# A new table of priorities for the list scheduler of a pooled attention and max-of-three feed-forward kernel

## The chip, the cores and the metric

The kernel runs on one core of a Trainium2 chip. The metric is the device time of one execution in microseconds; the kernel before takes 1482.36 us (median of 3 runs, 1482.32 to 1483.36). The engines are named as in the profile: PE (matmul; PEld loads its weights), DVE (VectorE), ACT (ScalarE), POOL (GpSimd), and SP, whose queue issues nearly all DMAs.

## The reference

Attention with queries averaged in pairs (1152 become 576), for 8 batches of 8 heads with 1152 keys and a head dimension of 64, and then a feed-forward stage on the 4608 resulting tokens, whose hidden layer is the maximum of three products:

```python
q_pool = q.reshape(B, H, S // factor, factor, D).mean(axis=3)
scores = scale * np.matmul(q_pool, k.transpose(0, 1, 3, 2))
scores = scores - np.max(scores, axis=-1, keepdims=True)
attn = np.exp(scores)
attn = attn / (np.sum(attn, axis=-1, keepdims=True) + 1e-09)
attn_out = np.matmul(attn, v)
...
h = np.maximum(np.maximum(x @ w1, x @ w2), x @ w3)
return (h @ w_out).astype(np.float32)
```

The weights w1, w2, w3 and w_out come as 64-bit floats, and the kernel turns each into a high and a low 32-bit part.

## The kernel before

**Units.** Attention is cut into 64 units, numbered d: a pair of heads (four pairs in each of 8 batches) and one half, 288, of its pooled queries. Scores lie with the keys on the partitions, in nine blocks of 128 keys. A unit goes through these steps, whose keys stand in the table of priorities:
- `qk` (lines 538 and 539): PE, four matmuls per key block into `pqk`, of which there are two buffers.
- `cp` (544): ACT copies `pqk` into a third of a tile `s`; a unit has three such tiles, and there are six buffers, so unit d takes those of unit d-2 over.
- `mx` (550, 553): DVE, running maximum `acc` over the key blocks, one buffer.
- `rows`, `red`, `bc` (589, 595, 605): PE transposes `acc` in five blocks (`pmt`), DVE reduces them, PE transposes the result back (`pmb`).
- `sub` (620) on DVE and `exp` (626) on ACT, six pieces each.
- `keys` (639, 641): POOL sums the exponentials over the key blocks into `ksum`, eight additions, in two buffers. The first addition of unit d waits until the `psum` of unit d-2 has read its buffer (line 644).
- `av` (669): PE, product with v into `pav`; `xcopy` (678) brings it to `xr`.
- `psum` (700 and 715 for d below 16, else 683): PE sums `ksum` over the partitions and spreads the reciprocals (`inv`, 690 and 710); `xm` (724 or 693) scales `xr`. `split` (768, 771) makes its high and low part.

**Feed-forward.** The tokens are cut into nine chunks, numbered from 0. Chunk b can start when the attention of its tokens is done; its steps are `mm` on PE, 216 matmuls `ph` (931; six blocks of the hidden layer, three weights each, four parts of 512 rows, three products of high and low parts), `evac` and `hhigh`/`hlow` (950, 952, 959, 962), then 72 matmuls `po` (986) and their copies and stores (1002, 1005). `mm` of all chunks stands in one chain (`tail`). `po` of chunk 0 waits for all six parts of w_out.

**Conversion.** With chunk 0, the weights are loaded (816), converted and stored for the later chunks (877), which fetch them (891). Of 24 conversions, `conv` in the table, 18 are of w1 to w3 (tiles `w0_0` to `w0_17`, four buffers, so `w0_4` waits until chunk 0 has used `w0_0`) and six of w_out (`wo_hi`, `wo_lo`). Each runs on ACT and DVE (831 to 858); the last two operations (861, 864) are POOL's for even numbers and DVE's, in two halves, for odd ones. `ph`, `po`, `psum`, the early `pav` and the conversions share two buffers `ff`.

**Order.** All steps go into a plan, and `arrange` walks through it with a clock for each engine: of the steps that are ready on the engine that is free first, it takes the one of lowest rank, and books an assumed duration. The instructions of each engine are then issued in this order; the chip waits on semaphores wherever a modelled time was too short. A step's rank is, with `at` near the unit's number d,

```python
lambda: at + R[key] + (R.get("first_" + key, 0) if at < 8 else 0) + NUDGE.get(name, 0)
```

and for the feed-forward steps of chunk b, with d the unit behind which it is planned (8, 16, ...) and i the place in the chunk,

```python
lambda: d + R["ffn"] + R[rate] * n * i / 576 + R[key] + NUDGE.get(name, 0)
```

`RANK` has an entry for each kind of step. `NUDGE` shifts single steps: those of units 0 to 19 (`keys.13`), and those of chunks 0 and 1 by eighths of 48 places (`conv.8.9`, `mm.8.3`). From unit 20 and chunk 2 on, `RANK` alone decides.

Of the kernel before, what the change touches and what calls it, by code (L numbers as in the profile page):

```python
# [36 lines left out]
    "qk": -94.8622,  # L37
    "cp": -198.877,
    "mx": -110.1936,
    "rows": -297.5399,  # L40
    "red": -97.7108,
    "bc": -69.2978,
    "sub": 36.0255,
    "exp": -154.9623,
    "keys": -14.5562,
    "av": 14.8431,
    "xcopy": -242.7422,
    "psum": 306.6745,
    "eps": 163.4791,
    "inv": 411.5164,  # L50
    "xm": -165.8669,
    "load": 11.9358,
    "prep": 513.6605,
    "move": 372.9744,
    "split": 31.5471,
    "ffn": -33.8173,
    "rate": 1.0394,
    "mm": 49.1178,
    "fetch": -156.7626,
    "evac": -234.7904,  # L60
    "hhigh": 172.1589,
    "hlow": -152.0307,
    "conv": 478.2091,
    "rate0": 4.4379,
    "first_qk": 87.3127,
    "first_cp": -260.4178,
    "first_mx": 25.0784,
    "first_sub": 35.563,
    "first_exp": 326.0935,
    "first_keys": -44.827,  # L70
    "first_av": 37.0199,
    "first_xcopy": -183.8483,
    "first_psum": -32.0782,
    "first_inv": -61.85,
    "first_xm": -117.3451,
    "first_load": -320.6766,
    "first_prep": -184.3904,
    "first_move": -506.8185,
    "first_split": 49.1161,
# [991 lines left out]
```

## Time and profile before

| | us |
|---|---|
| median of 3 runs | 1482.36 |
| lowest and highest run | 1482.32, 1483.36 |
| span of the profiled execution | 1480.9 |
| PE busy, 8704 matmuls | 1400.6 |
| POOL busy | 1078.7 |
| DVE busy | 1046.1 |
| ACT busy | 904.5 |

The profile gives the span of its execution, from the first to the last instruction, and no time of the whole execution; the median of the runs is 1.5 us above that span. Matmul ends are modelled, so a busy PE is not necessarily PE at its best. "Idle before" an instruction is put down to what ended it; a wait for several things is put down to the last of them. Which engine sets the pace changes during the span, so the tables by stretches say more than the shares.

### The profile page before, as it was taken

The page shows a single profiled execution, that of the slowest core. Times are in us where ns is not written, and L with a number is a line of the kernel's source. Part 1 is how long each engine was busy: PE and PEld are TensorE (multiplying, and loading weights), DVE is VectorE, ACT ScalarE, POOL GpSimd, SP SyncE. Part 2 cuts the span into 40 slices and gives each one's busy share as a digit, 9 for nine tenths or more (in the row PEclk, how much of TensorE's full clock was granted, in tenths as well). Part 3 has the DMA queues.
Part 4 walks back from the last instruction along what each step waited for, and adds up shares of the span by engine and source line. Part 5 has one row for each costly group of instructions (what it writes and reads, how often), then busy time and mean ns, then how long its engine had stood idle before and what let it go on. Part 6 is the DMA issues. An engine that isn't in the chain of part 4 may idle for free.

```text
span 1480.9 us, 24740 instructions
## 1 busy us (share of the span) xinstructions
PE 1400.6 (95%) x8704; PEld 1098.3 (74%) x8704; DVE 1046.1 (71%) x1441; ACT 904.5 (61%) x1464; POOL 1078.7 (73%) x835
## 2 busy tenths in 40 slices
PE   4788999888899999999999999999999999999999
PEld 4566666666567878778777777777777777778999
DVE  4898788989896875577777777877777778761110
ACT  4767766647676766467666676676766766651211
POOL 1888977686887868478887898789878988772210
PEclk9989899988999999999999999999999999999999
DMA  6556446657545665465566656664666556424441
GB/s 184 154 160 187 115 132 181 185 176 229 158 120 158 195 190 170 130 196 169 155 184 180 182 142 177 181 190 139 176 180 187 150 165 184 139 72 157 152 159 60
DMA packets 114762, 240.71 MB, mean 163 GB/s; under 512 B 15440, under 2 KB 75216, under 8 KB 114640
## 3 DMA queue, kind: packets, MB, share of 16 engines
q1 hardware_dynamic: 114064, 238.55, 55.2%
q8 instruction: 70, 1.15, 0.3%
q10 hardware_dynamic: 576, 0.59, 0.2%
q14 instruction: 52, 0.43, 0.1%
HBM read 144.70 MB, written 18.87 MB: 110 GB/s over the span
## 4 chain that ended last, share of the span: by engine, by line
PE 70%; DVE 4%; DMA 2%; issue 1%; POOL 1%; ACT 1%; SPq 0%; ACTq 0%; DVEq 0%
PE ph L931 27%; PE pav L669 13%; PE po L986 10%; PE pqk L538 7%; PE pqk L539 7%; PE pmt L589 2%; PE psum L683 2%; PE pmb L605 2%; DVE acc L553 1%; DMA w<-in_wout_dram 1%; DVE s L620 1%; DMA qq<-qraw 1%; POOL ksum L641 0%; DVE w L834 0%; DVE w L839 0%
## 5 line engine op out<-in xcount | busy, mean ns | idle before, releaser
L641 POOL TENSOR_TENSOR ksum<-ksum,s 128x576 f32<-128x576 f32 x448 | 638.0, 1424 | 28.9 <-ACT s L626 5.8
L931 PE MATMUL ph<-xh,w 128*128 128x512 f32 (+2 forms) x1440 | 464.6, 377 | 5.4 <-DVE hm L952 4.0
L620 DVE TENSOR_TENSOR s<-s,pmb 128x1035 f32<-128x1035 f32 (+1 forms) x384 | 396.9, 1049 | 46.0 <-PE pmb L605 46.0
L544 ACT COPY s<-pqk 128x576 f32<-128x576 f32 x576 | 362.5, 638 | 105.2 <-PE pqk L539 101.4
L538 PE MATMUL pqk<-qq,kc 128*128 128x288 f32 x1152 | 360.0, 327 | 57.1 <-DVE acc L553 35.3
L553 DVE TENSOR_TENSOR acc<-acc,pqk 128x576 f32<-128x576 f32 x448 | 335.3, 748 | 84.5 <-ACT s L544 81.7
L626 ACT ACTIVATE s<-s 128x1035 f32<-128x1035 f32 (+1 forms) x384 | 354.8, 934 | 60.2 <-DVE s L620 57.1
L539 PE MATMUL pqk<-qq,kc 128*128 128x288 f32 x1152 | 333.4, 304 | 0.0
L538 PEld LDWEIGHTS pqk<-qq,kc 128*128 128x128 f32 x1152 | 225.5, 196 | 113.5 <-DVE acc L553 51.7
L669 PE MATMUL pav<-s,v 128*64 128x288 f32 x2304 | 306.8, 419 | 1.8 <-DVE xr L724 1.4
L931 PEld LDWEIGHTS ph<-xh,w 128*128 128x128 f32 x1440 | 263.1, 188 | 45.9 <-DVE hm L952 4.9
L931 PE MATMUL ph<-xl,w 128*128 128x512 f32 (+2 forms) x720 | 268.4, 373 | 0.0
L669 PEld LDWEIGHTS pav<-s,v 128*64 128x64 f32 x2304 | 165.1, 141 | 122.0 <-issue 17.7
L539 PEld LDWEIGHTS pqk<-qq,kc 128*128 128x128 f32 x1152 | 227.9, 198 | 11.2
L962 POOL TENSOR_TENSOR h_lo<-hm,h_hi 128x512 fp32r<-128x512 f32 (+2 forms) x60 | 70.8, 1179 | 149.5 <-ACT h_hi L959 149.5
L639 POOL TENSOR_TENSOR ksum<-s 128x576 f32<-128x576 f32 x64 | 91.9, 1436 | 105.5 <-ACT s L626 103.1
L952 DVE TENSOR_TENSOR hm<-hm,ph 128x512 f32<-128x512 f32 (+2 forms) x120 | 75.4, 628 | 127.5 <-PE ph L931 127.5
L931 PEld LDWEIGHTS ph<-xl,w 128*128 128x128 f32 x720 | 135.8, 189 | 11.8
L595 DVE TENSOR_REDUCE m<-pmt 116x3 f32<-116x384 f32 (+1 forms) x128 | 61.1, 488 | 91.9 <-PE pmt L589 91.9
L434 POOL TENSOR_TENSOR kraw<-kraw 128x1152 fp32r<-128x1152 f32 x31 | 82.9, 2675 | 57.1 <-ACT kraw L430 39.4
L690 DVE RECIPROCAL rs<-rs 128x288 f32<-128x288 f32 (+1 forms) x64 | 96.3, 1506 | 18.5 <-ACT rs L687 18.2
L678 ACT COPY xr<-pav 128x288 f32<-128x288 f32 x64 | 25.4, 398 | 114.8 <-PE pav L669 114.6
(57 smaller groups left out, 1288.9 us busy)
## 6 DMA issues: line engine op xcount, KB each, us to landing
w<-w_split SPq DMA_DIRECT2D x144, 512.0 KB, 3.4
kc<-kraw SPq DMA_DIRECT2D x384, 96.0 KB, 2.3
qq<-qraw SPq DMA_DIRECT2D x252, 144.0 KB, 3.1
v<-in_vr_dram SPq DMA_DIRECT2D x32, 576.0 KB, 3.9
kraw<-in_kT_dram SPq DMA_DIRECT2D x31, 576.0 KB, 4.7
qraw<-in_qT_dram SPq DMA_DIRECT2D x31, 576.0 KB, 4.3
w<-in_win_dram SPq DMA_DIRECT2D x18, 512.0 KB, 4.8
w_split<-w SPq DMA_DIRECT2D x18, 512.0 KB, 4.9
```

What stands on the lines that cost most here:

```text
L538: nc.tensor.matmul(ps[:, h - hs[0], :QH], w, qq[:, 0, h], start=True, stop=False)
L539: nc.tensor.matmul(ps[:, h - hs[0], :QH], w, qq[:, 1, h], start=False, stop=True)
L544: nc.scalar.copy(o.s[kk // 3][:, kk % 3, slice(*hs)], o.ps[kk, hs][:, :, :QH])
L553: nc.vector.tensor_tensor(acc, acc, ps, op=ALU.max)
L620: nc.vector.tensor_tensor(s, s, o.pb[h][:, None, :w].broadcast_to([P, 3, w]), op=ALU.subtract)
L626: nc.scalar.activation(s, s, AF.Exp, scale=SCALE)
L639: vec[e].tensor_tensor(o.ksum, o.s[0][:, 0], x, op=ALU.add)
L641: vec[e].tensor_tensor(o.ksum, o.ksum, x, op=ALU.add)
L669: nc.tensor.matmul(o.pav[64 * h : 64 * h + 64, :QH], pr.v[:, kk, h], o.s[kk // 3][:, kk % 3, h], start=(kk == 0), stop=(kk == NK - 1),)
L690: nc.vector.reciprocal(o.rs, o.rs)
L931: nc.tensor.matmul(t.ps[:, : hi - lo], w[:, a, kk], xx[:, kk, lo:hi], start=(kk == 0 and i == 0), stop=(kk == 3 and i == 2),)
L986: nc.tensor.matmul(t.ps[:, : hi - lo], ww[:, kk, ms], hh[:, kk, lo:hi], start=(kk == 0 and i == 0), stop=(kk == 5 and i == 2),)
```

## The change

Nearly every number of `RANK` and `NUDGE` is another; the rest of the file is the same to the letter, and its lines stand four further down (L641 becomes L645). No instruction is added or removed. Some lines of the diff, with those that the prediction's places depend on:

```diff
 RANK = {
...
-    "keys": -14.5562,
+    "keys": -671.9276,
...
-    "conv": 478.2091,
+    "conv": 648.8915,
-    "rate0": 4.4379,
+    "rate0": 4.5084,
...
 NUDGE = {
...
-    "keys.13": 70.03, "keys.14": -1.58, "keys.15": 150.66, "keys.16": -24.33, "keys.17": -38.61,
...
+    "keys.10": 819.14, "keys.11": -128.29, "keys.12": -462.16, "keys.13": -32.25, "keys.14": 31.57,
...
-    "psum.11": -34.05, "psum.12": -38.59, "psum.13": 64.74, "psum.14": 8.12, "psum.15": 42.44,
...
+    "psum.10": -50.76, "psum.11": 93.35, "psum.12": -147.4, "psum.13": 122.83, "psum.14": 208.32,
```

Unit 13's `keys` had the rank 13 + 70.03 against 14 - 1.58 of unit 14 (with the same `RANK` entry in both); now it is 13 - 32.25 against 14 + 31.57.

What this does is seen in the order of instructions. In the first pair of rows DVE is at the end of the conversion of the last weight, `w64_23` into `wo_lo`. In the kernel before it reads

```order
L553 TENSOR_TENSOR acc19_3802<-acc19_3802,pqk19_8_3881 128x576
L834 TENSOR_SCALAR w64_105<-w64_23_0_3849 128x256
L834 TENSOR_SCALAR w64_105<-w64_23_256_3922 128x256
L839 SCALAR_TENSOR_TENSOR w64_23_0_3849<-w64_23_0_3849,w64_105 128x256
L839 SCALAR_TENSOR_TENSOR w64_23_256_3922<-w64_23_256_3922,w64_105 128x256
L844 TENSOR_SCALAR w64_23_0_3849<-w64_23_0_3849 128x256
L844 TENSOR_SCALAR w64_23_256_3922<-w64_23_256_3922 128x256
L847 SCALAR_TENSOR_TENSOR w64_105<-w64_105,w64_23_0_3849 128x256
L847 SCALAR_TENSOR_TENSOR w64_105<-w64_105,w64_23_256_3922 128x256
L861 TENSOR_TENSOR w64_23_0_3849<-w64_23_0_3849,wo_hi_103 128x256
L861 TENSOR_TENSOR w64_23_256_3922<-w64_23_256_3922,wo_hi_103 128x256
L864 TENSOR_TENSOR wo_lo_104<-w64_23_0_3849,w64_105 128x256
```

and in the changed kernel

```order
L868 TENSOR_TENSOR wo_lo_104<-w64_23_0_3758,w64_105 128x256
L848 TENSOR_SCALAR w64_23_256_3775<-w64_23_256_3775 128x256
L851 SCALAR_TENSOR_TENSOR w64_105<-w64_105,w64_23_256_3775 128x256
L599 TENSOR_REDUCE m18_0_3799<-pmt18_0_3786 116x3
L865 TENSOR_TENSOR w64_23_256_3775<-w64_23_256_3775,wo_hi_103 128x256
L599 TENSOR_REDUCE m18_1_3813<-pmt18_1_3801 116x2
L868 TENSOR_TENSOR wo_lo_104<-w64_23_256_3775,w64_105 128x256
L624 TENSOR_TENSOR s18_0_3590<-s18_0_3590,pmb18_0_3815 128x3x345
L624 TENSOR_TENSOR s18_0_3590<-s18_0_3590,pmb18_1_3828 128x3x231
L624 TENSOR_TENSOR s18_1_3674<-s18_1_3674,pmb18_0_3815 128x3x345
```

The last weight was finished after unit 19's running maximum (`acc19`); now it is finished ahead of unit 18's subtractions. The last `wo_lo` is instruction 573 of DVE before and 558 now, and on PE 66 fewer matmul instructions stand ahead of the first `po`.

The second pair is POOL at units 13 and 14. Before, `ksum14` stands ahead of `ksum13`:

```order
L639 TENSOR_TENSOR ksum14_2872<-s14_0_2610 128x576
L641 TENSOR_TENSOR ksum14_2872<-ksum14_2872,s14_0_2610 128x576
L641 TENSOR_TENSOR ksum14_2872<-ksum14_2872,s14_1_2664 128x576
L962 TENSOR_TENSOR h_lo0_1825<-hm0_3_2724,h_hi0_1824 128x512
L641 TENSOR_TENSOR ksum14_2872<-ksum14_2872,s14_1_2664 128x576 x2
L641 TENSOR_TENSOR ksum14_2872<-ksum14_2872,s14_2_2721 128x576 x3
L861 TENSOR_TENSOR w64_105<-w64_105,w0_14_2968 128x512
L864 TENSOR_TENSOR w0_14_2968<-w64_105 128x512
L639 TENSOR_TENSOR ksum13_3003<-s13_0_2429 128x576
L641 TENSOR_TENSOR ksum13_3003<-ksum13_3003,s13_0_2429 128x576
```

The changed kernel has

```order
L645 TENSOR_TENSOR ksum13_2821<-ksum13_2821,s13_2_2687 128x576
L865 TENSOR_TENSOR w64_105<-w64_105,w0_14_2873 128x512
L645 TENSOR_TENSOR ksum13_2821<-ksum13_2821,s13_2_2687 128x576
L868 TENSOR_TENSOR w0_14_2873<-w64_105 128x512
L645 TENSOR_TENSOR ksum13_2821<-ksum13_2821,s13_2_2687 128x576
L643 TENSOR_TENSOR ksum14_3018<-s14_0_2730 128x576
L645 TENSOR_TENSOR ksum14_3018<-ksum14_3018,s14_0_2730 128x576
```

Unit 13 is now summed first. On PE, the `psum11` that unit 13's sum waits for stood behind `ph0_4_1` and now stands behind `pqk13_3`.

The third pair is DVE in unit 12, where it takes the maximum over the key blocks (`acc12`) between the subtractions of unit 11 and the first feed-forward blocks (`hm0`). Before:

```order
L553 TENSOR_TENSOR acc12_2239<-acc12_2239,pqk12_2_2221 128x576
L620 TENSOR_TENSOR s11_1_2038<-s11_1_2038,pmb11_0_2214 128x3x345
L952 TENSOR_TENSOR hm0_1_2096<-hm0_1_2096,ph0_1_2_0_2232 128x512
L553 TENSOR_TENSOR acc12_2239<-acc12_2239,pqk12_3_2251 128x576
L620 TENSOR_TENSOR s11_1_2038<-s11_1_2038,pmb11_1_2228 128x3x231
L553 TENSOR_TENSOR acc12_2239<-acc12_2239,pqk12_4_2266 128x576
```

Now:

```order
L624 TENSOR_TENSOR s11_2_2105<-s11_2_2105,pmb11_0_2228 128x3x345
L624 TENSOR_TENSOR s11_2_2105<-s11_2_2105,pmb11_1_2233 128x3x231
L557 TENSOR_TENSOR acc12_2226<-acc12_2226,pqk12_2_2220 128x576
L557 TENSOR_TENSOR acc12_2226<-acc12_2226,pqk12_3_2245 128x576
L956 TENSOR_TENSOR hm0_2_2294<-hm0_2_2294,ph0_2_1_0_2289 128x512
L838 TENSOR_SCALAR w64_105<-w64_8_0_2309 128x512
L557 TENSOR_TENSOR acc12_2226<-acc12_2226,pqk12_4_2311 128x576
```

The maxima over `pqk12_2` to `pqk12_4` moved behind unit 11's subtractions, and the one over `pqk12_4` behind the block `ph0_2_1`, because PE now runs 30 matmuls of `ph` (the end of `ph0_1_2`, `ph0_2_0` and `ph0_2_1`) between `pqk12_3` and `pqk12_4`.

More of the change, by code (lines that the diff above doesn't have):

```diff
@@ L36 @@
 RANK = {
[L37 to L44, printed above, removed]
-    "keys": -14.5562,
-    "av": 14.8431,
[L47 to L55, printed above, removed]
-    "ffn": -33.8173,
[L57 to L62, printed above, removed]
-    "conv": 478.2091,
-    "rate0": 4.4379,
[L65 to L79, printed above, removed]
+    "qk": -364.0396,
+    "cp": -126.5549,
+    "mx": -318.2574,
+    "rows": -969.9796,
+    "red": -172.0313,
+    "bc": -345.8464,
+    "sub": 215.1752,
+    "exp": 196.9402,
+    "keys": -671.9276,
+    "av": 14.8431,
+    "xcopy": -516.1778,
+    "psum": 398.4083,
+    "eps": 343.2889,
+    "inv": 357.0576,
+    "xm": -706.0274,
+    "load": 386.6538,
+    "prep": 638.9001,
+    "move": 1290.4425,
+    "split": 283.1141,
+    "ffn": -33.8173,
+    "rate": 1.047,
+    "mm": 49.0387,
+    "fetch": 603.0832,
+    "evac": -724.5554,
+    "hhigh": 1228.3483,
+    "hlow": -714.7034,
+    "conv": 648.8915,
+    "rate0": 4.5084,
+    "first_qk": -97.1625,
+    "first_cp": -630.79,
+    "first_mx": 212.4188,
+    "first_sub": 204.5779,
+    "first_exp": 244.1512,
+    "first_keys": -1118.9276,
+    "first_av": 141.406,
+    "first_xcopy": -152.0387,
+    "first_psum": 65.359,
+    "first_inv": 141.5566,
+    "first_xm": 829.3378,
+    "first_load": -197.5173,
+    "first_prep": 180.1798,
+    "first_move": -1436.3679,
+    "first_split": 375.0794,
 }
 NUDGE = {
[77 rows of a table removed]
[81 rows of a table added]
 }
```

154 rows, old and new, of the table NUDGE are left out of this document.

## The prediction

> **What bounds the kernel now.** I read the page first, for which engine is full and when, and then the busy time in stretches of the span.
>
> ```profile
> PE 1400.6 (95%) x8704; PEld 1098.3 (74%) x8704; DVE 1046.1 (71%) x1441; ACT 904.5 (61%) x1464; POOL 1078.7 (73%) x835
> ...
> PE   4788999888899999999999999999999999999999
> ...
> DVE  4898788989896875577777777877777778761110
> ...
> POOL 1888977686887868478887898789878988772210
> PEclk9989899988999999999999999999999999999999
> ```
>
> The share over the span points to TensorE alone. By slices it is another story: in the first eleven (37 us each) PE is below nine tenths in most and its granted clock sags, while VectorE is at eight or nine. The table by stretches gives the numbers; its columns are the stretch, its length, then busy time of PE, PEld, DVE, ACT, POOL, the granted clock and DMA.
>
> ```profile
> 0.00:116.00 116.00, 83.77 (x499) 60.30 (x499) 83.62 (x134) 71.84 (x112) 73.36 (x58) 0.91 0.61 172
> 116.00:190.00 74.00, 65.17 (x479) 47.81 (x478) 54.28 (x82) 50.91 (x78) 65.66 (x48) 0.91 0.52 140
> 190.00:305.00 115.00, 101.66 (x663) 76.65 (x663) 105.28 (x178) 78.31 (x126) 80.25 (x58) 0.99 0.61 177
> 305.00:340.00 35.00, 30.41 (x181) 22.91 (x180) 28.68 (x61) 16.83 (x33) 26.68 (x20) 0.85 0.51 157
> 340.00:422.70 82.70, 67.79 (x410) 47.12 (x408) 74.82 (x126) 59.30 (x102) 71.10 (x59) 0.86 0.62 183
> 422.70:1480.90 1058.20, 1051.81 (x6482) 843.54 (x6480) 699.46 (x865) 627.33 (x1016) 761.64 (x596) 1.00 0.55 160
> ```
>
> Four regimes. To 116 us nothing is full for long. From 116 to 190 us POOL is (65.66 of 74.00, 89%). From 190 to 422.7 us DVE is: 92% in 190 to 305, 82% in 305 to 340, 90% in 340 to 422.7; here it carries the weight conversions beside the attention. From 422.7 us, where the first matmul of `po` of chunk 0 starts, PE is busy for 1051.81 of 1058.20 us at clock 1.00. The work is unchanged, so an order can win there only the 6.39 us of idle time, much of which is the last copy and store. **The end time is the time at which PE becomes full, plus the PE work then still to do.** Both terms are read at the start of that `po`.
>
> **Term 1: the last conversion comes sooner, with less PE work behind it.** Here is DVE at that point, and PE in the row below it.
>
> ```profile
> 419.67 0.75 DVE L864 TENSOR_TENSOR wo_lo<-w,w 128x256 fp32r<-128x256 f32 x2
> 420.33 0.88 DVE L595 TENSOR_REDUCE m<-pmt 116x3 f32<-116x384 f32 x2
> 421.55 1.23 DVE L620 TENSOR_TENSOR s<-s,pmb 128x1035 f32<-128x1035 f32 x1 [0.34 <-PE pmb L605]
> 422.70 0.75 DVE L550 TENSOR_TENSOR acc<-s,pqk 128x576 f32<-128x576 f32 x1
> 423.36 0.87 DVE L620 TENSOR_TENSOR s<-s,pmb 128x693 f32<-128x693 f32 x1
> ...
> 419.07 0.30 PE L538 MATMUL pqk<-qq,kc 128*128 128x288 f32 x1
> 419.21 0.30 PE L539 MATMUL pqk<-qq,kc 128*128 128x288 f32 x1
> ...
> 422.11 0.71 PE L683 MATMUL psum<-ksum,ones 128*64 128x288 f32 x4
> 422.75 0.51 PE L986 MATMUL po<-h_hi,wo_hi 128*128 128x512 f32 x1
> ```
>
> `po` needs all 24 converted weights; the last is ready at 420.4 us and `po` starts 2.3 us later. By the order, the last `wo_lo` is now DVE's instruction 558 instead of 573: 15 fewer stand ahead of it, namely one L550, seven L553, six L620 (three of each width) and one wide L690.
>
> ```profile
> L553 DVE TENSOR_TENSOR acc<-acc,pqk 128x576 f32<-128x576 f32 x448 | 335.3, 748 | 84.5 <-ACT s L544 81.7
> L620 DVE TENSOR_TENSOR s<-s,pmb 128x1035 f32<-128x1035 f32 x192 | 235.2, 1229 | 45.4 <-PE pmb L605 45.4
> L620 DVE TENSOR_TENSOR s<-s,pmb 128x693 f32<-128x693 f32 x192 | 166.6, 870 | 0.5 <-PE pmb L605 0.5
> L690 DVE RECIPROCAL rs<-rs 128x288 f32<-128x288 f32 x48 | 93.5, 1948 | 18.2 <-ACT rs L687 18.2
> L550 DVE TENSOR_TENSOR acc<-s,pqk 128x576 f32<-128x576 f32 x64 | 48.0, 750 | 18.1 <-ACT s L544 14.2 <-PE pmt L589 3.7
> ```
>
> 0.75 + 7 x 0.748 + 3 x (1.229 + 0.870) + 1.95 = 14.2 us. Durations overlap by 0.08 us where instructions follow each other (the L620 above takes 1.23 and its successor starts 1.15 later), so 15 of them occupy 13.0 us. If DVE stays 90% busy these are 14.4 us on the clock; I take the middle, 13.7 us earlier. What PE does ahead of `po` shrinks too, by about a unit: 36 matmuls of `pqk`, 36 records of `pav`, five `pmt`, five `pmb`, four `psum`. The `pqk` starts above are 0.14 apart; the chain of waits has the rest in its full part:
>
> ```profile
> 588.69 13.99 PE ph L931 x60
> ...
> 1321.24 0.50 PE pmb L605 x5
> 1321.74 7.59 PE po L986 x33
> 1329.33 4.51 PE pav L669 x36
> 1333.85 0.48 PE psum L683 x4
> ```
>
> 36 x 0.14 + 4.5 + 2 x 0.5 + 0.5 = 11.0 us (both kinds of transposes taken as 0.5). That work is not gone, it now follows the start of `po`. **Gain: 13.7 - 11.0 = 2.7 us.** If that cover failed, that is, if PE found nothing ready after `po` starts, it would be lost; but `po`'s 72 matmuls (16.6 us) and then chunk 1's `ph` lie ready, and by then every conversion is off DVE.
>
> **Term 2: the hole in unit 15 closes.** Three engines and PE, in order of time:
>
> ```profile
> 288.14 0.81 ACT L626 ACTIVATE s<-s 128x693 f32<-128x693 f32 x1
> ...
> 301.80 1.41 POOL L639 TENSOR_TENSOR ksum<-s 128x576 f32<-128x576 f32 x1 [3.70 <-ACT s L626]
> ...
> 317.36 2.25 PE L700 MATMUL psum<-ones,ksum 128*96 128x1 f32 x24
> ...
> 318.63 1.40 POOL L639 TENSOR_TENSOR ksum<-s 128x576 f32<-128x576 f32 x1
> ...
> 322.43 1.19 ACT L544 COPY s<-pqk 128x576 f32<-128x576 f32 x2
> ...
> 323.12 0.61 PE L538 MATMUL pqk<-qq,kc 128*128 128x288 f32 x1 [2.33 <-ACT s L544]
> ```
>
> The exponentials of unit 13 end at 288.95, yet POOL sums unit 14 at 301.80 and unit 13 only at 318.63: the sum of unit 13 may start once `psum11` has read the buffer of unit 11 (the wait on `chain` in line 644), and `psum11` stands on PE behind `ph0_4_1`, at 317.36. Unit 15's first copy needs tile `s` back from unit 13, so it runs at 322.43, and PE's next `pqk` at 323.12. In this hole DVE has conversions, but not enough: 6.3 us idle of 35. In the new order `psum11` follows `psum10` inside unit 13's `pqk`, and POOL sums unit 13 before unit 14. At the neighbouring stretches' 91% the idle time would be 3.1 us. **Gain: 3.2 us**; bounds 0 (another wait takes its place) and 6.3.
>
> **What may be paid.** New tight places on DVE. All 24 conversions still have to pass it, so a wait of DVE before 405 us is a wait of the kernel. The order puts three long runs of `ph` on PE between the score products: 30 between `pqk12_3` and `pqk12_4`, 24 ahead of `pqk13_2`, 18 ahead of `pqk14_5`, where before no run outside unit 15's hole exceeds 12. At 0.233 us each they are 7.0, 5.6 and 4.2 us. For the first I set both sides against each other, from unit 11's first reduction to the running maximum that wants `pqk12_4`:
>
> ```profile
> L952 DVE TENSOR_TENSOR hm<-hm,ph 128x512 f32<-128x512 f32 (+2 forms) x120 | 75.4, 628 | 127.5 <-PE ph L931 127.5
> ...
> L834 DVE TENSOR_SCALAR w<-w 128x256 uint32<-128x256 uint32 (+1 forms) x36 | 18.2, 511 | 8.4 <-ACT w L831 8.1 <-issue 0.3
> ```
>
> DVE: six L620 (6.3), three maxima (2.25), two L952 (1.26), a reduction (0.4, taken as half of the 0.88 for two), four conversion steps (2.0) = 12.2, less 16 x 0.08 = 10.9 us. PE: five `pmb` 0.5, eight `pqk` 1.1, 36 `ph` 8.4, and ACT's copy (0.6, half of the pair at 322.43) = 10.6 us. DVE is just covered; if it waits at all it is for a few tenths. Over the three runs I charge **1.0 us** (bounds 0 and half of 16.8, 8.4).
>
> **Taken as nothing.** The first conversions move forward into units 1 and 2 and their two loads go ahead of four `qq` moves on SP; up to unit 4 the same DVE work is done in both, in a stretch with DVE idle for 32 of 116 us. A loss or gain of up to 5 us lies in there; zero, since POOL is the fuller engine directly behind it, with the same work per unit. Behind `po`, units and chunks interleave otherwise until unit 32, where both orders have done the same PE work; PE is full, so nothing, within 3 us either way.
>
> **Sum.** 1480.9 - 2.7 - 3.2 + 1.0 = 1476.0 us of span. The profiled execution's span lies 1.5 below the median 1482.4, so 1477.5 us.
>
> Perfetto Trace Analysis of the Trainium skill (Identifying the Most-Contended Engine) would have the engine of highest occupancy improved first; read over the span, that is PE with 95%, whose work a reorder leaves as it is, which gives 1482.4 us, the first rival below. The same page (Optimization Strategy) allows for stretches with different engines in the lead, and the table above shows four; so I keep the sum.
>
> **The rivals.**
> - *No change, 1482.* PE's work is untouched, and the DVE-bound part only exchanges waits: terms 1 and 2 (5.9 us) are eaten by waits of DVE for the copies. DVE's waits from 190 to 423 us already sum to some 24 us, so 6 more are possible.
> - *Slower, 1488.* The three runs of `ph` make DVE wait for `pqk` behind them. Half of their 16.8 us is 8.4; if unit 15's hole does not close either (3.2), that is 1477.5 - 1.0 + 8.4 + 3.2 = 1488. It decides at the balance of 10.9 against 10.6 us: each us by which a conversion on POOL or a buffer of `ph` comes late passes through, since the `pqk` stand behind the run on PE. For it: the balance is that thin. Against it: POOL, which makes half of those weights, is busy for only 70% from 190 to 305 us.
> - *Faster still, 1470.* The whole 6.3 us of term 2 and 4 us of the early stretch are won.
>
> **How the numbers follow.** The forecast with its surroundings 0.45, faster still 0.10, no change 0.25, slower 0.20. A measurement of this kernel tells about 0.2% (3.0 us) from no change; part of the forecast's own spread falls inside that. Faster 0.54, same 0.26, slower 0.20. Predicted 1477.5, range 1467 to 1488.
>
> **What would show it.** Right: the first `po` starts at 405 to 411 us instead of 422.75, DVE is about 90% busy through 305 to 340 us, the copy of unit 15 no longer comes 30 us after unit 13's exponentials, and PE is full at clock 1.00 from then on. Wrong: DVE below 88% in 230 to 305 us with waits for the copies (the runs of `ph`), or PE idle after `po` has started.

## The result and the profile after

The changed kernel takes 1473.24 us (median of 6 runs, 1472.51 to 1479.94) against 1482.48 us before (6 runs, 1481.28 to 1483.36): a ratio of 0.9946 with a 95% interval from 0.9932 to 0.996, 9.2 us faster. The profiled execution took 1472.96 us, its span is 1471.1 us, 9.8 below that of before. First the page, with the same rows as before:

```profile
PE 1398.0 (95%) x8704; PEld 1098.5 (75%) x8704; DVE 1044.0 (71%) x1441; ACT 902.5 (61%) x1464; POOL 1079.1 (73%) x835
...
PE   4888999898899999999999999999999999999999
...
DVE  3897789898877767777688778777787768861110
...
POOL 1897975889868878679888878888787978772210
PEclk9988999998899999999999999999999999999999
```

Over the span nothing seems to have happened: the shares are those of before. The table by stretches of the changed kernel, cut at its own first `po` (columns as in the prediction), tells more:

```profile
0.00:116.00 116.00, 86.98 (x531) 63.07 (x531) 85.48 (x140) 73.81 (x115) 77.20 (x61) 0.94 0.66 184
116.00:190.00 74.00, 64.17 (x472) 47.25 (x472) 54.38 (x84) 51.23 (x78) 64.42 (x46) 0.90 0.50 130
190.00:305.00 115.00, 103.71 (x663) 80.12 (x663) 107.38 (x195) 76.56 (x128) 83.62 (x60) 0.97 0.57 176
305.00:340.00 35.00, 32.72 (x208) 25.43 (x207) 32.77 (x55) 26.89 (x47) 29.09 (x23) 0.96 0.88 261
340.00:393.93 53.93, 44.02 (x272) 30.62 (x270) 48.46 (x91) 35.37 (x63) 49.56 (x43) 0.78 0.54 152
393.93:1471.10 1077.17, 1066.39 (x6568) 851.97 (x6566) 715.57 (x882) 638.65 (x1034) 775.23 (x605) 1.00 0.55 160
```

Three things are to be seen. VectorE is busy for 32.77 of 35 us in 305 to 340 (28.68 before). The full stretch begins at 393.93 us instead of 422.75. And in the full stretch PE now stands still for 10.78 us, where it was 6.39. VectorE and PE at the last conversion, by the timeline of the changed kernel:

```profile
392.64 0.41 DVE L868 TENSOR_TENSOR wo_lo<-w,w 128x256 fp32r<-128x256 f32 x1
392.97 3.15 DVE L624 TENSOR_TENSOR s<-s,pmb 128x1035 f32<-128x1035 f32 x3
...
393.30 0.71 PE L687 MATMUL psum<-ksum,ones 128*64 128x288 f32 x4
393.93 0.51 PE L990 MATMUL po<-h_hi,wo_hi 128*128 128x512 f32 x1
```

To follow the gain through the span I take the start of the first `pqk` of five units, for all kernels of this study. At these units every order shown has issued the same matmuls, kind by kind (a dash where it has not), so a difference between two starts is a lead with equal work done on PE. These are readings of PE's timeline in each profiled execution, in us, named by the labels of the runs below:

| | unit 10 | unit 12 | unit 32 | unit 40 | unit 56 | span | unit 32 to the end |
|---|---|---|---|---|---|---|---|
| before | 188.1 | 226.9 | 687.7 | 845.7 | 1161.1 | 1480.9 | 793.2 |
| the change | 182.8 | 221.5 | 670.4 | 829.6 | 1149.1 | 1471.1 | 800.7 |
| e1 | 190.0 | 226.8 | 673.9 | 833.6 | 1148.8 | 1467.8 | 793.9 |
| e2 | 188.9 | 226.7 | 686.4 | 843.8 | 1158.0 | 1476.6 | 790.2 |
| e3 | 184.1 | 222.8 | 671.6 | 832.8 | 1148.9 | 1468.0 | 796.4 |
| e4 | 189.3 | 227.4 | - | 868.6 | 1182.8 | 1501.5 | - |
| e5 | 190.9 | 229.0 | 691.9 | 849.9 | 1165.1 | 1484.1 | 792.2 |
| e6 | 183.5 | 222.3 | 678.3 | 836.2 | 1152.0 | 1470.9 | 792.6 |
| e7 | 183.6 | 222.4 | 670.5 | 826.6 | 1138.7 | 1456.2 | 785.7 |
| e8 | 183.2 | 221.9 | 684.1 | 842.1 | 1156.5 | 1475.8 | 791.7 |
| e9 | 189.9 | 228.0 | 686.6 | 845.6 | 1163.8 | 1484.3 | 797.7 |
| e10 | 189.7 | 227.8 | 686.5 | 843.1 | 1156.5 | 1475.0 | 788.5 |
| e11 | 207.9 | 244.3 | - | 881.6 | 1193.6 | 1511.2 | - |

The change leads by 5.3 us at unit 10, by 17.3 at unit 32, and by 9.8 at the end. So it wins about 5 us where the prediction put none, some 12 where it put 4.9, and gives 7.5 back where it put none. Executions of one and the same order differ by some us (the change itself took 1472.5 to 1479.9), so a difference of 2 or 3 us in one cell proves nothing.

### The profile page after: what moved, and what is told of

It reads as the page before. It is cut to its first block, busy times and chain, and to the rows that moved or that the text cites. A ratio compares the mean times of both kernels' runs of the same rounds, so it can differ in the third digit from the quotient of the medians.

```text
span 1471.1 us, 24704 instructions
## 1 busy us (share of the span) xinstructions
PE 1398.0 (95%) x8704; PEld 1098.5 (75%) x8704; DVE 1044.0 (71%) x1441; ACT 902.5 (61%) x1464; POOL 1079.1 (73%) x835
## 4 chain that ended last, share of the span: by engine, by line
PE 75%; DVE 10%; DMA 4%; ACT 4%; issue 4%; POOL 2%; SPq 1%; ACTq 0%; DVEq 0%; POOLq 0%
PE ph L935 28%; PE pav L673 14%; PE po L990 10%; PE pqk L542 9%; PE pqk L543 8%; DVE s L624 3%; DVE acc L557 3%; DMA kraw<-in_kT_dram 2%; PE pmt L593 2%; PE psum L687 2%; PE pmb L609 2%; POOL ksum L645 1%; ACT s L548 1%; DVE w L848 1%; DVE w L843 1%
## 5 line engine op out<-in xcount | busy, mean ns | idle before, releaser
L645 POOL TENSOR_TENSOR ksum<-ksum,s 128x576 f32<-128x576 f32 x448 | 638.2, 1425 | 26.1 <-ACT s L630 3.5
L548 ACT COPY s<-pqk 128x576 f32<-128x576 f32 x576 | 362.4, 639 | 103.4 <-PE pqk L543 97.8
L624 DVE TENSOR_TENSOR s<-s,pmb 128x693 f32<-128x693 f32 (+1 forms) x384 | 395.1, 1049 | 39.5 <-PE pmb L609 38.3
L630 ACT ACTIVATE s<-s 128x693 f32<-128x693 f32 (+1 forms) x384 | 352.5, 933 | 41.9 <-DVE s L624 38.6
L694 DVE RECIPROCAL rs<-rs 128x288 f32<-128x288 f32 (+1 forms) x64 | 96.5, 1507 | 17.7 <-ACT rs L691 17.3
```

Source lines behind the costliest of these rows:

```text
L548: nc.scalar.copy(o.s[kk // 3][:, kk % 3, slice(*hs)], o.ps[kk, hs][:, :, :QH])
L624: nc.vector.tensor_tensor(s, s, o.pb[h][:, None, :w].broadcast_to([P, 3, w]), op=ALU.subtract)
L630: nc.scalar.activation(s, s, AF.Exp, scale=SCALE)
L645: vec[e].tensor_tensor(o.ksum, o.ksum, x, op=ALU.add)
L694: nc.vector.reciprocal(o.rs, o.rs)
```

## The experiments

**Halves of the two orders (e1, e2, e3, e8, e9).** Both tables stand in one file; the plan is arranged once with each, and the orders are joined at the first `pqk` of a unit:

```diff
+PARTS = [("old", 10), ("new", 32), ("old", None)]
...
+    tables = {"old": planned(*old), "new": planned(RANK_NEW, NUDGE_NEW)}
+    order, placed = [], set()
+    for table, unit in PARTS:
+        for s, e in tables[table]:
+            if unit is not None and s is qk[unit, 0]:
+                break
+            if s.index not in placed:
+                placed.add(s.index)
+                order.append((s, e))
```

e1 is as shown: only units 10 to 31 in the new order.

> Order of before up to the first score product of unit 10 and again from that of unit 32 on; between them the new order. At both cuts the two orders have done the same PE work. Theory A (the gain lies between units 10 and 32, where the hole of unit 15 closes and the table of PE work against time shows 12 us): 1470 us, 12 us under before. Theory B (the sum on record was right in its terms, 5.9 less 1.0 there, and the rest came from the early stretch): 1477 to 1478 us.

Measured: 1471.61 us (1469.38 to 1477.74), ratio 0.9931 (0.9911 to 0.9952), near the first theory. The middle alone, between two pieces of the old order, gives as much as the whole change. In the table it goes from 1.9 us behind at unit 10 to 13.8 ahead at unit 32. The middle is worth far more than the 4.9 us of the two terms.

e2 has `PARTS = [("new", 10), ("old", None)]`.

> New order up to the first score product of unit 10, then the order of before. Theory A: the early stretch, which the prediction took as nothing, is worth the 5.3 us that the traces show at unit 10, since everything behind it just moves: 1477 us. Theory B: POOL or DVE swallow it before PE is full, within 1 us of before (1481.5 to 1483.5).

Measured: 1477.06 us (1474.73 to 1478.87), ratio 0.9967 (0.9954 to 0.998). By the median the early stretch is worth 4.4 us. Its profiled execution doesn't show where: it is 3 us ahead at the start of unit 4 and behind at unit 10, and most of the lead that it ends with (3.0 of 4.3 us) arises behind unit 32, where its order is the old one. The other five executions with the new order up to unit 10 start that unit at 182.8 to 184.1, the six with the old order at 188.1 to 190.9, which speaks for the gain. About half of it can be seen in unit 3, first of the kernel before (62 to 82 us), then of the change (64 to 79.5):

```profile
62.00:82.00 20.00, 14.79 (x85) 10.48 (x84) 18.31 (x30) 13.11 (x23) 17.09 (x14) 0.74 0.51 132
```

```profile
64.00:79.50 15.50, 14.66 (x95) 9.61 (x95) 15.18 (x24) 12.65 (x22) 15.18 (x12) 1.00 0.71 198
```

In this unit VectorE now carries 7 steps of conversions instead of 13, since the first ones moved forward into unit 2. PE hardly pauses, and its clock stays at 1.00 instead of 0.74. The change starts unit 3 1.7 us later than the kernel before and unit 4 2.7 us earlier; where the rest of the 5.3 us at unit 10 comes from is open.

e3 has `PARTS = [("new", 32), ("old", None)]`.

> New order up to the first score product of unit 32, then the order of before. Theory A (the new order gives 7 to 8 us back behind unit 32, by a wait of ACT for a load that returns once in each chunk): 1465 to 1466 us, which beats both kernels. Theory B (the lead shrinks for a reason that no order changes): 1473 us, as the change.

Measured: 1473.63 us (1469.78 to 1475.44), ratio 0.9935 (0.9917 to 0.9954), no better than the change. The table says why: 4.0 of the 16.1 us of lead are gone between units 32 and 34, at the seam, where PE waits 3.1 us for a copy that stands on ACT behind the cast of a `kraw` still under way. From unit 34 (715.0 against 727.1 before, 12.1 us ahead) to the end (12.9 ahead) nothing more is lost. So the old order of the tail keeps a lead. The seam explains only part of the missed time: without its 4.0 us the median would be 1469.6, an estimate, and still above 1466; the profiled execution (1470.12 us) is one of the two fastest of the six.

e8 moves the seam: `PARTS = [("new", 24), ("old", None)]`.

> New order up to unit 24, old order from there on (the run with the seam at unit 32 lost 4 us at the seam itself and nothing behind unit 34). Theory A (the old order of the tail gives nothing back, and the 4 us were an accident of the seam): span 1463 to 1465, 1465 to 1469 us. Theory B (a lead of some 17 us can't be kept by any order of the tail, because loads or POOL don't keep up): span 1467 to 1471, 1470 to 1474 us.

Measured: 1480.73 us (1477.88 to 1485.57), ratio 0.9992 (0.9979 to 1.0004). Neither theory's time, and again the seam. The first `po` starts at 393.4 us, as in the change, but at unit 32 the lead is 3.6 us instead of 17.3. Behind the joint the busy table has this, with VectorE and ACT waiting for each other in turns:

```profile
493.00:532.00 39.00, 33.20 (x177) 25.76 (x178) 28.80 (x36) 24.95 (x37) 28.81 (x21) 0.82 0.47 126
```

From unit 32 on it needs 791.7 us, as the other old tails do (790.2 to 793.9, without e3, whose seam lies in this stretch). A joint between two good orders can cost 13 us, so the times of joined kernels say little, and their stretches away from the joint much.

e9 is the mirror, `PARTS = [("old", 32), ("new", None)]`.

> The mirror of the third run: old order up to unit 32, new order behind it. Theory A (the new order of the tail costs 7 to 8 us against the old one whatever stands ahead of it, because casts of kraw hold ACT): 1488 to 1491 us, with PE waiting for acc behind runs of ph. Theory B (only a kernel that arrives early loses them): 1481 to 1484 us.

Measured: 1489.39 us (1486.1 to 1491.28) against 1482.23, ratio 1.0048 (1.0032 to 1.0063). The new order of the tail costs time also behind the old head: 7.2 us by the medians, though only 4.5 in the profiled execution (797.7 against 793.2 from unit 32), which is the fastest of the six. PE's waits in 690 to 1300 us (waited for, total, times, longest) in this run:

```profile
PE pqk L668 <- DVE acc L680: 5.1, 4, 1.4
```

and in the change:

```profile
PE pqk L542 <- DVE acc L554: 6.5, 4, 1.9
```

The kernel before has no such wait there. What lies behind it is in the chain of waits of the change:

```profile
705.34 0.51 ACT rs L691
705.85 0.09 SPq L1009
...
706.12 6.92 DMA kraw<-in_kT_dram
...
713.30 1.15 ACT kraw L434
714.45 0.55 ACT s L548
...
715.02 0.77 DVE acc L554
...
715.83 0.40 PE pqk L542
```

The load of a `kraw` goes out on SP behind a store and lands 6.92 us later. ACT, which has done other work until 711.5, has its cast (L434) next in line and stands for 1.8 us; behind it waits the copy of a `pqk` (L548), for the copy VectorE's maximum, and for that PE's next `pqk`.

**One number (e4).** The kernel before, with one `NUDGE`:

```diff
-    "psum.11": -34.05, "psum.12": -38.59,
+    "psum.11": -434.05, "psum.12": -38.59,
```

> The kernel before with one number changed, the nudge of psum.11 from -34.05 to -434.05. Its order is that of before up to unit 14; the columns of psum 11 come 20 us earlier on PE, POOL sums unit 13 ahead of unit 14, and po of chunk 0 moves ahead of unit 20. Theory A (the late psum 11 is the cause of the hole, and terms 1 and 2 both hang on it): 1470 to 1476 us. Theory B (the hole is filled by conversions anyway, so only its 3 us of idle time can be won and may be lost again): 1479 to 1483 us.

Measured: 1506.22 us (1503.28 to 1506.63), ratio 1.0157 (1.0138 to 1.0177): 24 us slower, against both theories. Everything behind unit 14 was planned anew. By the trace, unit 15 does lose its hole (it takes 18.7 us instead of 45.3, with 15 us less PE work in it), and units 16 and 17 take, beyond their PE work, 32 us more than before. There ACT's timeline reads

```profile
386.15 0.72 ACT L831 ACTIVATE w<-w 128x256 f32<-128x256 f32 x2 [5.41 <-DMA w<-in_wout_dram]
387.71 0.70 ACT L858 CAST wo_hi<-w 128x256 fp32r<-128x256 f32 x2 [0.84 <-DVE w L839]
388.31 1.19 ACT L544 COPY s<-pqk 128x576 f32<-128x576 f32 x2
...
395.73 0.72 ACT L831 ACTIVATE w<-w 128x256 f32<-128x256 f32 x2 [4.72 <-DMA w<-in_wout_dram]
```

and PE, in 345 to 405 us, waits behind it:

```profile
PE pqk L538 <- ACT s L544: 11.6, 1, 11.6
```

As in the tail, the copies of the scores stand in line behind an instruction that waits for a load. But here the load doesn't land late, it goes out late. The chain of waits has

```profile
381.69 0.43 DVE wo_lo L864
382.15 3.98 DMA w<-in_wout_dram
```

and 3.98 us is nearly what the planner books for its 512 KB (512 / 250 + 1.8 = 3.8). SP holds it back until VectorE's last step of an earlier conversion (L864) is done. As a test of the hole this run is worthless, since it changed too much.

**The hole alone (e5).** So the order of before was edited by hand, at this place only: `psum11` with its reciprocal and its scaling follows `psum10`, and the sums of units 13 and 14 with their `psum` change places.

```diff
+    order = swap(order)
...
+    put(cols, named("xm.10")[0])
+    put(first, cols)
+    put(second, first)
+    put(spread, red13[0])
+    put(scale, spread)
+    put(mm, bc13[1])
...
+    for key in ("keys", "psum", "inv", "xm"):
+        for x, y in zip(named(f"{key}.13"), named(f"{key}.14")):
+            i, j = seq.index(x), seq.index(y)
+            seq[i], seq[j] = y, x
```

> The kernel before with its own order, edited by hand in one place and not planned anew: psum11 with its reciprocal and scaling follows psum10, and the sums of units 13 and 14 (and the psum of both) change places. Theory A (term 2 of the prediction: the hole of unit 15 is worth 3 to 6 us by itself): 1476 to 1479 us, span 1475 to 1478. Theory B (closing it by itself gains nothing, VectorE's stream loses the time again right behind it): 1481 to 1483 us.

Measured: 1484.84 us (1481.31 to 1486.83), ratio 1.0016 (1.0006 to 1.0026). Nothing is gained. The sum of unit 13 now ends at 320.5 us, yet the copy that was to wait for it comes no sooner. This run at that place, by the chain of waits:

```profile
323.74 0.95 PE psum L731 x12
...
325.15 0.74 PE psum L746 x12
```

and ACT by its timeline:

```profile
326.40 0.40 ACT L862 ACTIVATE w<-w 128x256 f32<-128x256 f32 x1 [1.43 <-DVE xr L755]
327.20 0.37 ACT L889 CAST w<-w 128x256 fp32r<-128x256 f32 x1 [0.40 <-DVE w L870]
327.47 1.19 ACT L575 COPY s<-pqk 128x576 f32<-128x576 f32 x2
```

The copy (327.47) stands on ACT behind a conversion step, which waits for one of the two `ff` buffers, which a `psum` at the end of PE's run of `ph` still holds. The kernel before has the same, ahead of its copy at 322.43:

```profile
320.80 0.40 ACT L831 ACTIVATE w<-w 128x256 f32<-128x256 f32 x1 [4.73 <-DVE xr L724]
```

The step waits for 4.73 us, until the scaling (L724) has read the `psum`. So the late sum that the prediction followed was not what held the copy, or not alone. The edit has two limits. Before, the `psum` of units 11 and 14 stand together at the end of PE's run of `ph` (the 24 matmuls at 317.36 in the prediction); in e5 that of unit 13 stands in the place of unit 14's, so the buffer's part was not taken away. And ACT's own order was left as it was, with the copy behind these conversion steps. So e5 shows that an early sum alone gains nothing in this order, not what an order planned around it would gain.

**The casts later (e6).** The change, with each cast of a `kraw` from unit 24 on three ACT instructions later:

```diff
+        casts.append((r, x[-1], ks[-1]))
...
+    for r, cast, low in casts:
+        if r >= FROM:
+            i = next(n for n, x in enumerate(order) if x[1] is cast)
+            moved = [order.pop(i)]
+            n = 0
+            while n < LATER and low not in order[i][1].after and cast not in [a for a in order[i][1].after if order[i][1] is not low]:
+                if order[i][1] is low:
+                    moved.append(order.pop(i))
+                else:
+                    n += order[i][2] == "act"
+                    i += 1
+            order[i:i] = moved
```

> The changed kernel, with one edit by hand behind unit 24: ACT's cast of each kraw stands three ACT instructions later. Theory A (of the 17.3 us that the change leads by at unit 32, 7.5 are lost because this cast waits for its load and holds ACT's copies of the scores behind it): 1466 to 1469 us, and PE's waits for acc between 700 and 1300 us gone. Theory B (they are lost to something else in the new order of the tail): 1472 to 1474 us.

Measured: 1471.86 us (1467.57 to 1472.95), ratio 0.9922 (0.9908 to 0.9937), between the theories and next to the second. The trace separates them: from unit 32 to the end 792.6 us instead of 800.7, the level of the old tails, and PE's waits for `acc` from 690 to 1300 us fall from 6.5 to 0.7 us. Its execution lost elsewhere: at unit 15, ahead of the edit and in an order equal to the change's, it is 5 us later than the change (308.2 against 303.1). Another 2.7 us are lost between units 24 and 32, where the edit is already at work.

**An honest landing time (e7, e10, e11).** The planner books a load's landing at its size over 250 plus 1.8 us, 4.1 us for the 576 KB of a `kraw`. The profile has for this load (count, size, median us to landing), in the change

```profile
kraw<-in_kT_dram SPq DMA_DIRECT2D x31, 576.0 KB, 6.0
```

and before

```profile
kraw<-in_kT_dram SPq DMA_DIRECT2D x31, 576.0 KB, 4.7
```

The fit for a single DMA in the Trainium skill (SBUF — State Buffer, The DMA setup-cost knee: 2 us plus the bytes over 436 GB/s) would make it 3.4 us, an estimate that none of these medians agrees with; the measured ones are used. e7 is the change with

```diff
-            s.tail = wire - s.end + 1.8
+            s.tail = wire - s.end + (1.8 if t < 450 else 4.4)
```

so that the order up to some 450 us stays as it is.

> The changed kernel, with the planner's assumed landing time of a load 2.6 us longer from its time 450 us on; the order ahead of that is the same, the rest is planned anew. Theory A (casts planned too close behind their loads): 1466 to 1469 us. Theory B (the loss is of another kind): 1472 to 1475 us. As the run with one number showed, planning anew can bring waits of its own; above 1475 us it would be that.

Measured: 1458.1 us (1458.03 to 1462.15, 4 runs), ratio 0.9841 (0.9825 to 0.9857): 24 us faster than before, 15 faster than the change, and beyond both theories. The busy table from 690 to 1300 us, for the kernel before, the change and e7 in turn:

```profile
690.00:1300.00 610.00, 606.95 (x3766) 471.98 (x3766) 467.46 (x572) 411.28 (x649) 507.07 (x390) 1.00 0.59 168
```

```profile
690.00:1300.00 610.00, 602.55 (x3727) 465.80 (x3724) 464.93 (x568) 407.61 (x645) 493.61 (x376) 1.00 0.59 166
```

```profile
690.00:1300.00 610.00, 610.00 (x3814) 477.17 (x3811) 476.04 (x580) 419.27 (x663) 507.92 (x391) 1.00 0.57 168
```

In e7 PE has no pause at all in these 610 us, and it issues 48 more matmuls than before. At the place where the change stood, ACT of e7 does the copies first and meets a load that has landed:

```profile
713.24 0.64 ACT L548 COPY s<-pqk 128x576 f32<-128x576 f32 x1 [0.29 <-PE pqk L543]
713.88 1.07 ACT L630 ACTIVATE s<-s 128x1035 f32<-128x1035 f32 x1
714.86 1.14 ACT L434 CAST kraw<-kraw 128x1152 fp32r<-128x1152 f32 x1
```

So both the 7.5 us that the change gave back and 7.5 us that the kernel before had lost all along (785.7 against 793.2 from unit 32) were to be had. That the cast is the cause is shown for the first part alone, by e6; e7 plans everything behind 450 us anew, and what it gains beyond e6 (785.7 against 792.6) has no single cause that a run shows. A plan made anew with another assumption, as a control, was not run.

e10 is the same edit in the kernel before.

> The kernel before, with the planner's assumed landing time 2.6 us longer from its time 450 us on (the edit of the run that took 1458 us, on the old table). Theory A (that edit mends what the new table broke in the tail, and the old table's tail had no such waits): 1480 to 1484 us. Theory B (the old tail too hides 7 us that its full PE doesn't show, as 24.7 against 17.3 us of lead in that run suggest): 1473 to 1477 us.

Measured: 1477.49 us (1474.99 to 1480.09), ratio 0.9968 (0.9958 to 0.9979), between the two theories and nearer to the second: the old tail did hide time, 4.7 us of it by the edit (788.5 instead of 793.2 from unit 32). It shows in ACT's waits at the cast of `kraw` in 690 to 1300 us, before

```profile
ACT kraw L430 <- DMA qq<-qraw: 23.4, 9, 5.1
```

and in the change

```profile
ACT kraw L434 <- DMA qq<-qraw: 17.6, 7, 4.9
```

(the profile names the load that landed last). In e6, e7 and e10 no wait at this cast is listed. In the kernel before PE's idle time in this stretch is only 3.05 us.

e11 is the change with 4.4 in place of 1.8 from the start.

> The changed kernel with the longer landing time in the plan from the start. Theory A (loads land later than planned in the head too, where the weights come in; an honest time helps there as well): 1450 to 1457 us. Theory B (the new table's numbers fit the old assumption up to 450 us, and planning the head anew opens holes, as one number did to the old table): 1462 us or more.

Measured: 1514.76 us (1512.42 to 1518.8), ratio 1.0223 (1.0202 to 1.0245), as the second theory had it. The head planned anew is 25 us behind the change at unit 10 already. The starts drift apart in units 5 and 6, which take 55.5 us instead of 30.8; what causes it there is open. The numbers of the table go with the assumption under which they were found, and in this run a truer assumption under the same numbers made a worse plan.

## Why the prediction was right in the sum and wrong in two of its terms

The time lies inside the range, 4.3 us below the forecast of 1477.5 (0.9946 against 0.997), and on the side that had the highest chance. By its own terms, with the two profiled executions, in us:

| term | forecast | measured |
|---|---|---|
| early stretch, up to unit 10 | 0, within 5 | -5.3 |
| unit 10 to the last `wo_lo`: less work on VectorE | -13.7 | -15.9 |
| the same stretch: idle time of VectorE | -3.2 + 1.0 | -6.2 |
| from the last `wo_lo` to `po` | 0 | -1.4 |
| PE work moved behind `po` | +11.0 | +10.8 |
| behind `po` | 0, within 3 | +8.2 |
| sum | -4.9 | -9.8 |

The second and third rows come from VectorE's busy time, before in

```profile
188.10:420.40 232.30, 199.89 (x1259) 146.88 (x1257) 206.82 (x360) 155.02 (x261) 177.63 (x135) 0.92 0.60 176
```

and after in

```profile
182.80:393.00 210.20, 184.86 (x1180) 140.67 (x1179) 190.96 (x345) 141.86 (x243) 167.60 (x129) 0.92 0.61 183
```

206.82 - 190.96 = 15.9 us less work (15 instructions fewer, as counted), and (232.30 - 206.82) - (210.20 - 190.96) = 6.2 us less idle. The PE work ahead of `po` is an estimate, with each kind of matmul at its spacing in the full stretch: 10.6 us with medians, 11.2 with means that take in the waits, and the row behind it moves with it.

- **What bounds it.** "The end time is the time at which PE becomes full, plus the PE work then still to do" held as a frame. Its corollary failed: "an order can win there only the 6.39 us of idle time". e7 needs 7.5 us less than before from unit 32 on alone, the changed order 7.5 us more, and e9 shows such a loss behind the old head. PE at 99.4% busy still lost time: for the same 4894 matmuls from unit 32 on it is busy for 782.35 us in e7, 786.81 before and 789.92 in the change, so part of what an order loses is booked as busy time.
- **Term 1** was right in its mechanism and near in its size: 15 instructions, 15.9 us against 13.7, with about 11 us of PE work moved behind, as forecast. The durations of VectorE's instructions in the two stretches add up to 228.2 and 214.0 us, 14.2 less, the forecast's own sum. That the busy time fell by 1.6 more comes from instructions that overlap their predecessors further, which the forecast did not have.
- **Term 2** had the right sign and a cause that was not shown to be one. VectorE's idle time in 305 to 340 us fell from 6.3 to 2.2 us, 4.1 against the forecast 3.2 and inside its bounds; within unit 15 itself it fell from 6.9 to 1.7 us. But e5, which lets the sum of unit 13 come early, gains nothing. The step that failed is the chain from `psum11` over the sum to the copy: the copy had a second thing to wait for, a conversion step ahead of it on ACT without a buffer, and that one came as late. Which part of the new order closes the hole is open; e4 closed it too, and lost more behind.
- **The charge of 1.0 us** for the long runs of `ph` wasn't needed: VectorE is busy for 107.38 of 115 us in 190 to 305, more than the 105.28 before, and its idle time in units 12 to 14, where the runs stand, is 6.5 us against 6.1. The slower rival, which hung on these runs, fell.
- **The early stretch** was mis-sized: taken as nothing, it gave 5.3 us in the profile and 4.4 by the median of e2. The reason given, POOL as the fuller engine right behind, didn't absorb it.
- **Behind `po`** was the failed step that mattered: "PE is full, so nothing, within 3 us". 8.2 us were given back, 7.5 of them from unit 32 on. e3 and e9 speak for the order of the tail; the chain of waits and e6 show that it is the cast of `kraw` ahead of the copies.
- **The signs.** VectorE was 94% busy in 305 to 340 us, and 91% in 230 to 305. The copy of unit 15 came 9.9 us after unit 13's exponentials (304.01 against 294.15; before 33.5). The first `po` came at 393.93, earlier than the 405 to 411 named. One sign of being wrong did appear: PE idle after `po` has started.
- **One reading was loose.** In the first eleven slices VectorE is not at eight or nine throughout; two of them are a four and a seven. Nothing in the sum hangs on it.
- **The rivals.** No change, the reading by the shares over the span, fell with the interval; the measured time lies between the forecast and the faster rival (1470), whose early gain did come.

The middle gave some 8 us more than forecast, the early stretch 5 more, and the tail took 8: the forecast came as near as it did by luck, because errors of both signs met. Without the tail's loss the change would have taken some 1465 us, an estimate from 1473.24 and 8.2, below the range.

## What to carry to other kernels

In these traces an engine that waited for a load held up all that stood behind it in its order. Look in the trace for the instruction that waits for a DMA, and put work that others wait for ahead of it. The Trainium skill (DMA: Bandwidth & Descriptors, Rules for kernel authors) says to issue a DMA early and to wait on its semaphore late. e6 and e7 agree: with the cast later, PE's 6.5 us of waits for `acc` in the tail fell to 0.7 us in e6 and to none in e7. An engine that is busy for 99% of a stretch is no proof that an order can't win there; compare the time for equal work between two orders, which showed 785.7, 793.2 and 800.7 us here. A planner's table and its assumptions belong together: the landing time that won 15 us in the tail lost 41 us where it also replanned the head, and one number in the table lost 24.

## What was not expected of the hardware

The loads of `kraw`, 576 KB each, landed in medians of 4.3 us (e10) to 6.0 us (the change) in different orders of the same work, and in 6.92 us where the chain of waits shows one. And pauses of PE cost more than their length: in e8's 39 us at the seam PE was busy for 33.20 us, so it paused for 5.8, none of the pauses over 1.6 us. But e8 came to unit 32 12.5 us after e3, which has the same order up to unit 24 and no pause of PE between units 24 and 32. The granted clock was 0.82 in these 39 us. Matmuls of `pqk` that started 0.13 us apart at 496.5 us started 0.24 apart at 504.5.
